# Neighborhood attention on one core: one two-bank P V tile per pair, and another division of work in the last step

## The chip, the cores and the metric

The kernel runs on one core of a Trainium2 chip. A core has five engines with queues of their own: TensorE (PE, with its weight loads shown as PEld), VectorE (DVE), ScalarE (ACT), GpSimd (POOL) and SyncE (SP). Each works its instructions off in the order in which they stand, and waits for others by semaphores. DMAs are issued from the queues of SP, ACT and POOL. Matmul results land in PSUM (eight banks of 2 KB a partition), which ACT and DVE read. The metric is the device time of one execution in microseconds.

## The reference

Every pixel of a 224 x 224 image with 192 channels attends to a 7 x 7 neighborhood with dilation 2, with a single head over all channels:

```python
qkv = x @ wqkv
off = jnp.arange(7) * 2
r0 = jnp.clip(ir - 6, 0, H - 1 - 12)          # ir, ic: row and column numbers; c0 likewise
ri = r0[:, None] + off[None, :]
nidx = (ri[:, None, :, None] * W + ci[None, :, None, :])
logits = jnp.einsum('bnc,bnkc->bnk', qf, kn) * C ** (-0.5)
p = softmax(logits)
o = jnp.einsum('bnk,bnkc->bnc', p, vn) @ wo
```

`kn` and `vn` are the rows of k and v that `nidx` names. Near the borders the window is clipped, so that the first and last rows and columns share windows. Inputs and outputs are bfloat16.

## The kernel before

**Tiling.** The dilation splits rows and columns by parity, and rows are handled by parity class `rc`. A step works on 16 rows of one class over the whole width; there are 14 steps (`NSTEP`), the classes taking turns. The width of a step is cut into 14 slots (`NSLOT`) of eight column pairs. Two slots make a pair (`class Pair`, called a job's pair in the title): m = 0 to 6 in a step n, k = 0 to 97 over all, with `ab` = 0 or 1 for the slot in the pair. The key projection is folded into the query side (G), the output projection into the values (VF, VD), so there is no separate projection of the output.

**Stages of a pair.** `stage1` makes the scores in PSUM by 16 or more matmuls a pair and the negative maxima on DVE (L503); `stage1b` makes the exponentials on ACT (L511, four a pair). `stage2` transposes the exponentials on PE into one PSUM tile (L521) and copies it to SBUF as `pt_sb` (L523, "the PT copy" below). `stage3` multiplies by the values (L532, P V matmuls), and since the values carry a column of ones, columns 192 and 193 of the result hold the sums of the exponentials. `stage4a` takes the reciprocals (L538); `stage4` normalizes into `o_sb` or, for slot 0, `o_s0` (L552 on DVE, L550 on ACT), and issues the stores (L558, and L571 for slot 0, "left-edge stores").

**The loop.** The body runs for k = 0 to 99. In one pass the engines get the scores and the maxima of pair k, the P V matmuls of pair k - 2 and their normalization, the transposes and the PT copy of pair k - 1, and between these the projections of the next step: `w64` (left-over half groups of G, in the passes m = 0, 2, 4 and 6) and `w128` (whole groups of G, and values). The last step has no projections to make. `in_order(tc)` fixes the order on each engine as it stands in the code, so no scheduler moves anything.

On DVE a pass is: two reductions, reciprocal and normalization of slot 0 of pair k - 2, PT copy of pair k - 1, reciprocal and normalization of slot 1 of pair k - 2. In the last step the PT copies of pairs 0 to 4 are on ACT. For the last three pairs the second slot's normalization is on ACT, as two operations, one for each column class.

**Buffers.** `ps_o` has two PSUM banks, one for each slot's P V result; `ps_t` one for the transposes, `ps_g` three for projections, weight preparation and the tiles of the last pair. `o_sb` has six tiles of one slot, `o_s0` two. A tile is given again when its last reader in the order of the code has been issued, and the new writer waits for the reader's semaphore: for a store, its landing.

**Stores.** A slot has a run of 16 rows, or in the last step one of 13 rows and one of 3 (the clipped rows have another spacing). Long runs go to SP's queue. Short runs go to POOL's or SP's by slot, and in the last two slots to ACT's at the end (`end_q`). The left-edge stores, ten or more for a step, wait in `pool_q`, together with POOL's copies of the next band (`sort_items`, `xb_items`); `pool_do` issues up to four of that list at the end of each pass. POOL also copies half groups of G out of `gx` (L460), for which it waits on ACT.

Of the kernel before, what the change touches and what calls it, by code (L numbers as in the profile page):

```python
# [8 lines left out]
BF = mybir.dt.bfloat16  # L9
F32 = mybir.dt.float32  # L10
# [11 lines left out]
NSLOT = 14  # L22
# [76 lines left out]
def kernel(  # L99
# [15 lines left out]
    pers = ctx.enter_context(tc.tile_pool(name="pers", bufs=1))  # L115
    ps_s = ctx.enter_context(tc.tile_pool(name="ps_s", bufs=1, space=PSUM))
    ps_t = ctx.enter_context(tc.tile_pool(name="ps_t", bufs=1, space=PSUM))
    ps_o = ctx.enter_context(tc.tile_pool(name="ps_o", bufs=2, space=PSUM))
    ps_g = ctx.enter_context(tc.tile_pool(name="ps_g", bufs=3, space=PSUM))
    x1_p = ctx.enter_context(tc.tile_pool(name="x1", bufs=2))  # L120

# [182 lines left out]
            nc.gpsimd.memset(_win(t, 0, 128, 112 * rc, [[128, 8], [1, 16]]), 0.0)  # L304
    wT_lo = setup.tile([128, 3, C], BF, name="wT_lo")
    wT_hi = setup.tile([64, 3, C], BF, name="wT_hi")
    n_t = 0
    for X in range(3):
        for (dt_, d0, dn) in ((wT_lo, 0, 128), (wT_hi, 128, 64)):
            tp = (ps_o, ps_g)[n_t % 2].tile([128, 1024], BF, name="tp_w", tag=("o", "pg")[n_t % 2])  # L310
            n_t += 1
            nc.tensor.transpose(tp[0:dn, 0:128], w_lo[:, X * C + d0: X * C + d0 + dn], ident[:])
            nc.tensor.transpose(tp[0:dn, 128:192], w_hi[:, X * C + d0: X * C + d0 + dn], ident[0:64, 0:64])
            nc.scalar.copy(out=dt_[:, X, :], in_=tp[0:dn, 0:192])
# [90 lines left out]
    def g_items(rc, ti, s0, ns):  # L405
# [41 lines left out]

        def halves(dve, direct=False):
            pg = ps_g.tile([128, 512], F32, name="pgh", tag="pg")
            pg1 = ps_o.tile([128, 512], F32, name="pgh", tag="o") if direct else pg  # L450
            both(mm(pg, 0, XDAT[0], OUT_B[0]), mm(pg1, 1, XDAT[1], OUT_B[1]))
            if direct:
                put(G[rc][0], (NSLOT + s0) * 128, pg, False, XDAT[0], 64)
                put(G[rc][1], (NSLOT + s0) * 128, pg1, True, XDAT[1], 64)
                return
            gx = work.tile([128, 512], BF, name="gx", tag="gx", bufs=3)
            put(gx, 0, pg, dve)
            for cc in range(2):
                p = XDAT[cc]
                nc.gpsimd.tensor_copy(out=G[rc][cc][p:p + 64, 1, s0:s0 + ns, :], in_=gx[p:p + 64, 0:ns * 128].rearrange("p (s q) -> p s q", q=128))  # L460
# [50 lines left out]
            nc.scalar.activation(out=J.p[:, ab, cc, :, z:z + 112].rearrange("p q (r k) -> p q r k", k=8), in_=_win(s_ps, 0, 128, cc * 256, [[8, 2], [16, 14], [1, 8]]),  # L511
                                 func=ACTF.Exp, bias=nmx[:, cc:cc + 1], scale=1.0)

    def stage2(J):
        pool_ = ps_t if J.k < NP - 1 else ps_g
        pt_ps = pool_.tile([128, 8, 128], BF, name="pt_ps", tag="pt" if J.k < NP - 1 else "pg")
        for ab in range(2):
            for cc in range(2):
                for q in range(2):
                    for h in range(2):  # L520
                        nc.tensor.transpose(pt_ps[64 * h:64 * h + 64, 4 * ab + 2 * cc + q, :], J.p[:, ab, cc, q, 64 * h:64 * h + 64], ident[:])  # L521
        J.pt = work.tile([128, 8, 128], BF, name="pt_sb", tag="pt_sb")
        (nc.scalar.copy if J.n == NSTEP - 1 and J.m < 5 else nc.vector.tensor_copy)(out=J.pt[:], in_=pt_ps[:])  # L523

    def stage3(J, ab):
        rc, s = J.rc, 2 * J.m + ab
        o_ps = (ps_o if J.k < NP - 1 else ps_g).tile([128, 512], F32, name="o_ps", tag="o" if J.k < NP - 1 else "pg")
        V = (VD[rc], VF[rc])
        for cc in range(2):
            for q in range(2):  # L530
                for h in range(2):
                    nc.tensor.matmul(o_ps[64 * h:64 * h + 64, cc * 193:cc * 193 + 193], lhsT=J.pt[:, 4 * ab + 2 * cc + q, 64 * h:64 * h + 64],  # L532
                                     rhs=V[h][:, (s - 1 + q) % NSLOT, cc * C:cc * C + 193], start=(q == 0), stop=(q == 1))
        J.o_ps[ab] = o_ps

    def stage4a(J, ab):
        J.rs[ab] = stat.tile([128, 2], F32, name="rs", tag="rs")
        nc.vector.reciprocal(out=J.rs[ab][:], in_=J.o_ps[ab][:, C:C + 2])  # L538
        return J.rs[ab]

    def stage4(J, ab):
        rc, ti, s, o_ps = J.rc, J.ti, 2 * J.m + ab, J.o_ps[ab]
        rs = J.rs.get(ab) or stage4a(J, ab)
        if s > 0:
            o_sb = work.tile([128, 2, C], BF, name="o_sb", tag="o_sb", bufs=6)
        else:
            o_sb = work.tile([128, 2, C], BF, name="o_s0", tag="o_s0")
        if J.k >= NP - 3 and ab == 1:
            for cc in range(2):
                nc.scalar.mul(o_sb[:, cc, :], o_ps[:, 194 * cc:194 * cc + C], rs[:, cc:cc + 1])  # L550
        else:
            nc.vector.tensor_tensor(out=o_sb[:], in0=_win(o_ps, 0, 128, 0, [[194, 2], [1, C]]),  # L552
                                    in1=rs[:].unsqueeze(2).to_broadcast([128, 2, C]), op=ALU.mult)
        prow = _rows(rc, ti)
        if s > 0:
            for (j0, nj, r0, rstep) in _aff_runs(prow):
                def put(eng, j0=j0, nj=nj, r0=r0, rstep=rstep):
                    eng.dma_start(out=op[r0: r0 + (nj - 1) * rstep + 1: rstep, 8 * s - 3:8 * s + 5, :],  # L558
                                  in_=o_sb[8 * j0:8 * (j0 + nj)].rearrange("p t c -> p (t c)"))

                if nj < 8 and J.n == NSTEP - 1 and s > 11:
                    end_q.append(put)
                else:
                    put(nc.gpsimd if nj < 8 and (s % 2 == 1 if J.n == 0 else s not in (3, 6, 9)) else nc.sync)
            return
        for h in range(2):
            for (j0, nj, r0, rstep) in _aff_runs(prow[8 * h:8 * h + 8]):
# [7 lines left out]
    for n, (ti, rc) in enumerate(steps):  # L575
        for m in range(7):
            J = Pair()
            J.n, J.ti, J.rc, J.m, J.k, J.o_ps, J.s, J.rs = n, ti, rc, m, len(pairs), {}, {}, {}
            pairs.append(J)
    NP = len(pairs)  # L580

# [5 lines left out]
    act, dve, pool = nc.scalar.copy, nc.vector.tensor_copy, nc.gpsimd.tensor_copy  # L587
    pool_q = []
    end_q = []

    def pool_do(n):
        for _ in range(min(n, len(pool_q))):
            pool_q.pop(0)()
# [35 lines left out]
    for k in range(NP + 2):  # L629
# [18 lines left out]
            if m == 0 and n + 3 < NBAND:  # L648
                ld = load_items(n + 3)
        if k == NP:  # L650
            stage2(pairs[k - 1])
        if k >= 2:
            stage3(pairs[k - 2], 0)
            stage3(pairs[k - 2], 1)
            if k >= NP:
                stage4a(pairs[k - 2], 0)
                stage4a(pairs[k - 2], 1)
            stage4(pairs[k - 2], 0)
            if k == NP - 1:
                stage4a(pairs[k - 2], 1)  # L660
        for it in w64:
            it(False)
        if J:
            stage1b(J, 1)
        if 1 <= k < NP:
            stage2(pairs[k - 1])
        if k >= 2:
            stage4(pairs[k - 2], 1)
        if not J:
            continue  # L670

# [46 lines left out]
        if n == 12 and m == 1:  # L718
# [1 line left out]
            g_col(1, 6, 0, 1, pool)  # L720
            g_row(1, 6, 0, 1, pool, last)
            g_row(1, 6, 1, 13, pool, last[1:])
        pool_do(4 if n + 1 < NSTEP else 3)
    pool_do(len(pool_q))
    for it in end_q:
        it(nc.scalar)
    in_order(tc)


# [28 lines left out]
```

## Time and profile before

| | |
|---|---|
| median of 3 runs | 364.18 us (363.53 to 366.75) |
| the profiled execution | 362.85 us, span 361.1 us, granted TensorE clock 0.996 |
| busy: PE / PEld | 335.6 / 305.8 us |
| busy: DVE / ACT / POOL | 313.7 / 307.5 / 285.6 us |
| normalizations on DVE (L552) | 193, 557 ns each |
| reciprocals (L538) | 196, 159 ns each |
| PT copies | 93 on DVE, 686 ns; 5 on ACT, 1018 ns |
| left-edge stores on POOL (L571) | 150 of 162 shown under one name, 568 ns to issue each |

The table's durations are those of single instructions; DVE and ACT overlap the end of one with the start of the next by about 0.1 us. A busy PE is modelled, since matmuls are pipelined. SP's queue has no busy time in the page; its instructions are seen in the order of time.

### The profile page before, as it was taken

To read this page: it belongs to the slowest core of one execution; us is meant where nothing else is said; L and a number is where in the kernel's file an instruction comes from. 1 tells how busy PE (TensorE), PEld (TensorE's weight loads), DVE (VectorE), ACT (ScalarE), POOL (GpSimd) and SP (SyncE) were. 2 spreads that over 40 slices of the span, in tenths; PEclk is the share of its full clock that TensorE was granted. 3 is DMA by queue.
4 is the path that set the end of the run, shared out by engine and by line. 5 is a ranking of instruction groups with operands and counts; after the bars stand their busy time and mean duration, and the time that the engine had idled before them with its cause. 6 is when DMAs were issued, how large, how long until landed. Compare 5 with 4: busy or idle time off the path is not lost.

```text
span 361.1 us, 19455 instructions
## 1 busy us (share of the span) xinstructions
PE 335.6 (93%) x8104; PEld 305.8 (85%) x8104; DVE 313.7 (87%) x743; ACT 307.5 (85%) x821; POOL 285.6 (79%) x456
## 2 busy tenths in 40 slices
PE   3988888998999999999999999999999999999881
PEld 1676777997999899999989999899999999999671
DVE  8967987887998998989989999898998889989992
ACT  3654767997998999989999999999989989999792
POOL 8976799999896986959969699696995878374094
PEclk9999999999999999999999999999999999999998
DMA  9999986697988979899799998988989965634432
GB/s 188 204 175 180 174 172 148 146 199 162 202 177 201 196 164 190 186 194 192 168 183 181 197 190 177 161 213 180 198 178 192 191 146 121 143 97 108 103 80 77
DMA packets 137778, 60.79 MB, mean 168 GB/s; under 512 B 88841, under 2 KB 137166, under 8 KB 137691
## 3 DMA queue, kind: packets, MB, share of 16 engines
q1 hardware_dynamic: 130133, 56.37, 78.3%
q0 software_dynamic: 5520, 1.73, 2.7%
q10 hardware_dynamic: 2038, 1.47, 2.2%
q8 instruction: 63, 1.03, 1.2%
q14 instruction: 24, 0.20, 0.2%
HBM read 0.29 MB, written 19.27 MB: 54 GB/s over the span
## 4 chain that ended last, share of the span: by engine, by line
PE 69%; POOL 10%; DVE 8%; ACT 6%; DMA 3%; issue 2%; SPq 1%; POOLq 0%; DVEq 0%; ACTq 0%
PE pv L345 16%; PE s L501 15%; PE o_ps L532 14%; PE pg L425 10%; PE pt_ps L521 9%; PE pgh L425 5%; POOL out_dram L571 4%; ACT p L511 3%; DVE xb L160 2%; POOL xs L170 2%; POOL out_dram L558 2%; DMA out_dram<-o_sb 1%; DMA vd<-vf 1%; ACT vf L335 1%; DVE nmx L503 1%
## 5 line engine op out<-in xcount | busy, mean ns | idle before, releaser
L511 ACT ACTIVATE p<-s,nmx 128x224 bf16<-128x224 f32 x392 | 149.8, 450 | 24.5 <-DVE nmx L503 22.8
L503 DVE TENSOR_REDUCE nmx<-s 128x2 f32<-128x392 f32 (+1 forms) x196 | 102.4, 564 | 19.9 <-PE s L501 19.4
L552 DVE TENSOR_TENSOR o_sb<-o_ps,rs 128x384 bf16<-128x384 f32 x179 | 99.8, 557 | 7.1 <-DMA out_dram<-o_sb 0.9
L460 POOL COPY g<-gx 64x512 bf16<-64x512 bf16 (+1 forms) x110 | 61.8, 562 | 52.9 <-ACT gx L335 47.1
L345 PE MATMUL pv<-wp,xs 128*64 128x192 bf16 x1624 | 92.7, 250 | 7.1 <-POOL xs L170 1.9
L345 PEld LDWEIGHTS <-xs 128*64 128x64 bf16 x1624 | 78.5, 111 | 20.5 <-issue 8.8
L335 ACT CAST vf<-pv 128x384 bf16<-128x384 f32 x193 | 87.6, 518 | 9.6 <-PE pv L345 5.2
L571 POOL DMA_DIRECT2D out_dram<-o_s x150 | 84.2, 568 | 1.1 <-issue 1.1
L532 PE MATMUL o_ps<-vd,pt_sb 128*64 128x193 bf16 x784 | 82.2, 246 | 2.9 <-ACT pt_sb L523 2.1
L501 PE MATMUL s<-xa,g 128*64 128x196 bf16 (+7 forms) x990 | 82.2, 233 | 1.6 <-issue 0.5
L532 PE MATMUL o_ps<-vf,pt_sb 128*64 128x193 bf16 x784 | 82.1, 246 | 0.0
L501 PE MATMUL s<-xb,g 128*64 128x196 bf16 (+7 forms) x990 | 81.8, 232 | 0.3 <-ACT g L335 0.3
L501 PEld LDWEIGHTS <-g 128*64 128x64 bf16 x1980 | 77.6, 110 | 3.6 <-issue 2.5
L532 PEld LDWEIGHTS <-pt_sb 128*64 128x64 bf16 x1568 | 71.3, 109 | 4.9 <-ACT pt_sb L523 3.2
L523 DVE COPY pt_sb<-pt_ps 128x1024 bf16<-128x1024 bf16 x93 | 63.7, 686 | 5.4 <-PE pt_ps L521 0.6
L521 PE MATMUL pt_ps<-ident,p 128*64 128x128 bf16 x1568 | 63.9, 219 | 0.0
L521 PEld LDWEIGHTS <-p 128*64 128x64 bf16 x1568 | 57.0, 110 | 5.2
L335 ACT CAST g<-pg 128x512 bf16<-128x512 f32 (+4 forms) x136 | 57.6, 471 | 2.0 <-PE pg L425 2.0
L425 PEld LDWEIGHTS <-aw 128*64 128x64 bf16 x1320 | 54.1, 110 | 4.1 <-issue 0.7
L425 PE MATMUL pg<-xb,aw 128*64 128x512 bf16 (+9 forms) x440 | 53.9, 269 | 0.6 <-DVE xb L160 0.6
L425 PE MATMUL pg<-xa,aw 128*64 128x512 bf16 (+9 forms) x440 | 52.0, 270 | 0.0
L170 POOL COPY xs<-xa 128x896 bf16<-128x896 bf16 x50 | 45.1, 928 | 1.4
(75 smaller groups left out, 282.8 us busy)
## 6 DMA issues: line engine op xcount, KB each, us to landing
vd<-vf SPq DMA_DIRECT2D x49, 336.9 KB
out_dram<-o_sb SPq DMA_DIRECT2D x156, 96.0 KB
out_dram<-o_sb SPq DMA_DIRECT2D x26, 78.0 KB
out_dram<-o_s POOLq DMA_DIRECT2D x78, 9.0 KB, 3.9
vd<-vf SPq DMA_DIRECT2D x2, 337.8 KB
vd<-vf ACTq DMA_DIRECT2D x2, 336.9 KB
xa<-in_x_dram SPq DMA_TRANSPOSE x28
out_dram<-o_s POOLq DMA_DIRECT2D x26, 15.0 KB, 3.1
```

What stands on the lines that cost most here:

```text
L335: nc.scalar.copy(out=out_, in_=in_)
L345: nc.tensor.matmul(pv[64 * h:64 * h + 64, cc * C:(cc + 1) * C], lhsT=at(k, h), rhs=WP[(cc, pas)][:], start=(pas == 0), stop=(pas == 1))
L425: nc.tensor.matmul(o, lhsT=l, rhs=r, start=(pas == 0), stop=(pas == 1))
L460: nc.gpsimd.tensor_copy(out=G[rc][cc][p:p + 64, 1, s0:s0 + ns, :], in_=gx[p:p + 64, 0:ns * 128].rearrange("p (s q) -> p s q", q=128))
L501: nc.tensor.matmul(o, lhsT=w, rhs=r, start=(pas == 0), stop=(pas == 1))
L503: nc.vector.tensor_reduce(out=nmx[:], in_=_win(s_ps, 0, 128, lo, [[256, 2], [16, 14], [1, 16 - lo]]), axis=AX.XY, op=ALU.max, negate=True)
L511: nc.scalar.activation(out=J.p[:, ab, cc, :, z:z + 112].rearrange("p q (r k) -> p q r k", k=8), in_=_win(s_ps, 0, 128, cc * 256, [[8, 2], ...
L521: nc.tensor.transpose(pt_ps[64 * h:64 * h + 64, 4 * ab + 2 * cc + q, :], J.p[:, ab, cc, q, 64 * h:64 * h + 64], ident[:])
L523: (nc.scalar.copy if J.n == NSTEP - 1 and J.m < 5 else nc.vector.tensor_copy)(out=J.pt[:], in_=pt_ps[:])
L532: nc.tensor.matmul(o_ps[64 * h:64 * h + 64, cc * 193:cc * 193 + 193], lhsT=J.pt[:, 4 * ab + 2 * cc + q, 64 * h:64 * h + 64], rhs=V[h][:, ( ...
L552: nc.vector.tensor_tensor(out=o_sb[:], in0=_win(o_ps, 0, 128, 0, [[194, 2], [1, C]]), in1=rs[:].unsqueeze(2).to_broadcast([128, 2, C]), op ...
L571: pool_q.append(lambda dst=dst, p=p, m=n * nj, cc=cc: nc.gpsimd.dma_start(out=dst.rearrange("j i c -> i j c"), in_=o_sb[p:p + m, cc, :]))
```

## The change

1. A pair's two slots share one PSUM tile of two banks, and `ps_o` holds a single one of them (same banks as before). One reciprocal of 128 x 4 and one normalization of 128 x 768 (reading both banks) stand in place of two each, ahead of the PT copy. `o_sb` becomes a tile of both slots, with four buffers; `o_s0` is gone, so the left-edge half lies in the pair's tile. The weight preparation at the start uses `ps_g` alone.
2. In the last step the outputs of all slots are kept in `XS[0]`, which is free by then, so no output buffer is given again. The PT copies of that step are on ACT in the passes m = 2 and 4, and on DVE in the others. In the passes m = 1, 3, 5, 6 and in the two after the last pair, the normalization is split: slot 0 on DVE, slot 1 on ACT; otherwise it is the joint one on DVE.
3. The short runs of the last step are stored for several slots at once: when slot 9 is done, three stores on POOL, one for each row, with slots 1 to 9; when slot 13 is done, three with slots 10 to 13, on ACT, SP and ACT.

```diff
-    ps_o = ctx.enter_context(tc.tile_pool(name="ps_o", bufs=2, space=PSUM))
+    ps_o = ctx.enter_context(tc.tile_pool(name="ps_o", bufs=1, space=PSUM))
...
-            tp = (ps_o, ps_g)[n_t % 2].tile([128, 1024], BF, name="tp_w", tag=("o", "pg")[n_t % 2])
+            tp = ps_g.tile([128, 1024], BF, name="tp_w", tag="pg")
...
-        (nc.scalar.copy if J.n == NSTEP - 1 and J.m < 5 else nc.vector.tensor_copy)(out=J.pt[:], in_=pt_ps[:])
+        eng(out=J.pt[:], in_=pt_ps[:])
...
+    def stage3(J):
+        rc = J.rc
+        if J.k < NP - 1:
+            o = ps_o.tile([128, 2, 512], F32, name="o_ps", tag="o")
+            J.o_ps = [o[:, ab, :] for ab in range(2)]
+            J.o_2 = o
+        else:
+            J.o_ps = [ps_g.tile([128, 512], F32, name="o_ps", tag="pg") for ab in range(2)]
...
     def stage4a(J, ab):
...
+        if J.rs is None:
+            J.rs = stat.tile([128, 2, 2], F32, name="rs", tag="rs")
+            if J.n < NSTEP - 1:
+                J.o_sb = work.tile([128, 2, 2, C], BF, name="o_sb", tag="o_sb", bufs=4)
+            else:
+                J.o_sb = _win(XS[0], 0, 128, 4 * C * J.m, [[2 * C, 2], [C, 2], [1, C]])
+        if ab is None:
+            nc.vector.reciprocal(out=J.rs[:], in_=_win(J.o_2, 0, 128, C, [[512, 2], [1, 2]]))
         else:
-            o_sb = work.tile([128, 2, C], BF, name="o_s0", tag="o_s0")
-        if J.k >= NP - 3 and ab == 1:
+            nc.vector.reciprocal(out=J.rs[:, ab, :], in_=J.o_ps[ab][:, C:C + 2])
+
+    def stage4b(J, ab, eng):
+        if ab is None:
+            nc.vector.tensor_tensor(out=J.o_sb[:], in0=_win(J.o_2, 0, 128, 0, [[512, 2], [194, 2], [1, C]]),
+                                    in1=J.rs[:].unsqueeze(3).to_broadcast([128, 2, 2, C]), op=ALU.mult)
+        elif eng is nc.vector:
+            nc.vector.tensor_tensor(out=J.o_sb[:, ab], in0=_win(J.o_ps[ab], 0, 128, 0, [[194, 2], [1, C]]),
+                                    in1=J.rs[:, ab, :].unsqueeze(2).to_broadcast([128, 2, C]), op=ALU.mult)
+        else:
             for cc in range(2):
+                nc.scalar.mul(J.o_sb[:, ab, cc, :], J.o_ps[ab][:, 194 * cc:194 * cc + C], J.rs[:, ab, cc:cc + 1])
...
+                if J.n < NSTEP - 1:
+                    put(nc.gpsimd if nj < 8 and s % 2 == 1 else nc.sync)
+                elif nj >= 8:
+                    put(nc.sync)
+                elif s in SHORT:
+                    for j in range(nj):
+                        def row(eng, p=8 * (j0 + j), r=r0 + j * rstep, a=SHORT[s]):
+                            eng.dma_start(out=op[r, 8 * a - 3:8 * s + 5, :].rearrange("(t i) c -> i t c", i=8),
+                                          in_=_win(XS[0], p, 8, 2 * C * a, [[2 * C, s + 1 - a], [1, 2 * C]]))
+                        if s < NSLOT - 1:
+                            pool_q.append(lambda row=row: row(nc.gpsimd))
+                        else:
+                            end_q.append(row)
...
+    SHORT = {9: 1, NSLOT - 1: 10}
...
+            P = pairs[k - 2]
+            stage3(P)
+            split = n == NSTEP or n == NSTEP - 1 and m % 2 == (0 if m == 6 else 1)
+            if P.k < NP - 1:
+                stage4a(P, None)
+            else:
+                stage4a(P, 0)
+                stage4a(P, 1)
+            stage4b(P, 0 if split else None, nc.vector)
+            stage5(P, 0)
...
         if 1 <= k < NP:
-            stage2(pairs[k - 1])
+            stage2(pairs[k - 1], act if n == NSTEP - 1 and m in (2, 4) else dve)
         if k >= 2:
-            stage4(pairs[k - 2], 1)
+            if split:
+                stage4b(P, 1, nc.scalar)
+            stage5(P, 1)
...
-        pool_do(4 if n + 1 < NSTEP else 3)
+        pool_do(4)
     pool_do(len(pool_q))
-    for it in end_q:
-        it(nc.scalar)
+    for it, eng in zip(end_q, (nc.scalar, nc.sync, nc.scalar)):
+        it(eng)
```

More of the change, by code (lines that the diff above doesn't have):

```diff
@@ L306 @@
     wT_hi = setup.tile([64, 3, C], BF, name="wT_hi")
-    n_t = 0
     for X in range(3):
         for (dt_, d0, dn) in ((wT_lo, 0, 128), (wT_hi, 128, 64)):
-            tp = (ps_o, ps_g)[n_t % 2].tile([128, 1024], BF, name="tp_w", tag=("o", "pg")[n_t % 2])
-            n_t += 1
+            tp = ps_g.tile([128, 1024], BF, name="tp_w", tag="pg")
             nc.tensor.transpose(tp[0:dn, 0:128], w_lo[:, X * C + d0: X * C + d0 + dn], ident[:])
@@ L449, in halves @@
             pg = ps_g.tile([128, 512], F32, name="pgh", tag="pg")
-            pg1 = ps_o.tile([128, 512], F32, name="pgh", tag="o") if direct else pg
+            pg1 = ps_o.tile([128, 2, 512], F32, name="pgh", tag="o")[:, 0, :] if direct else pg
             both(mm(pg, 0, XDAT[0], OUT_B[0]), mm(pg1, 1, XDAT[1], OUT_B[1]))
@@ L512, in stage1b, with stage2 @@
                                  func=ACTF.Exp, bias=nmx[:, cc:cc + 1], scale=1.0)
-    def stage2(J):
+    def stage2(J, eng):
         pool_ = ps_t if J.k < NP - 1 else ps_g
@@ L522, in stage2 @@
         J.pt = work.tile([128, 8, 128], BF, name="pt_sb", tag="pt_sb")
[L523 to L527, printed above, removed]
-        V = (VD[rc], VF[rc])
[L529 to L534, printed above, removed]
@@ L536, in stage4a @@
-    def stage4a(J, ab):
[L537 to L545, printed above, removed]
-        else:
-            o_sb = work.tile([128, 2, C], BF, name="o_s0", tag="o_s0")
-        if J.k >= NP - 3 and ab == 1:
+        eng(out=J.pt[:], in_=pt_ps[:])
@@ new lines, in stage3 @@
+    def stage3(J):
[6 more added lines that the diff above has]
+            J.o_ps = [ps_g.tile([128, 512], F32, name="o_ps", tag="pg") for ab in range(2)]
+        V = (VD[rc], VF[rc])
+        for ab in range(2):
+            s = 2 * J.m + ab
+            for cc in range(2):
+                for q in range(2):
+                    for h in range(2):
+                        nc.tensor.matmul(J.o_ps[ab][64 * h:64 * h + 64, cc * 193:cc * 193 + 193], lhsT=J.pt[:, 4 * ab + 2 * cc + q, 64 * h:64 * h + 64],
+                                         rhs=V[h][:, (s - 1 + q) % NSLOT, cc * C:cc * C + 193], start=(q == 0), stop=(q == 1))
@@ L549, in stage4, with stage5 @@
             for cc in range(2):
[L550 to L553, printed above, removed]
+                nc.scalar.mul(J.o_sb[:, ab, cc, :], J.o_ps[ab][:, 194 * cc:194 * cc + C], J.rs[:, ab, cc:cc + 1])
+    def stage5(J, ab):
+        rc, ti, s, o_sb = J.rc, J.ti, 2 * J.m + ab, J.o_sb[:, ab]
@@ L559, in put @@
                                   in_=o_sb[8 * j0:8 * (j0 + nj)].rearrange("p t c -> p (t c)"))
[L561 to L564, printed above, removed]
+                if J.n < NSTEP - 1:
[11 more added lines that the diff above has]
+                            end_q.append(row)
             return
@@ L577 @@
             J = Pair()
-            J.n, J.ti, J.rc, J.m, J.k, J.o_ps, J.s, J.rs = n, ti, rc, m, len(pairs), {}, {}, {}
+            J.n, J.ti, J.rc, J.m, J.k, J.s, J.rs = n, ti, rc, m, len(pairs), {}, None
             pairs.append(J)
@@ L650 @@
         if k == NP:
-            stage2(pairs[k - 1])
+            stage2(pairs[k - 1], dve)
         if k >= 2:
[L653 to L660, printed above, removed]
+            P = pairs[k - 2]
[8 more added lines that the diff above has]
+            stage5(P, 0)
         for it in w64:
@@ L665 @@
         if 1 <= k < NP:
-            stage2(pairs[k - 1])
+            stage2(pairs[k - 1], act if n == NSTEP - 1 and m in (2, 4) else dve)
         if k >= 2:
-            stage4(pairs[k - 2], 1)
+            if split:
+                stage4b(P, 1, nc.scalar)
+            stage5(P, 1)
         if not J:
```

## The prediction

> **What bounds the kernel now.** I read the busy times by stretch first, then the waits of TensorE (PE), then the order on VectorE (DVE), the POOL queue, and last the end of the SP queue. The busy times by stretch (start:end and length in us, then busy us of each engine; 0 to 66 left out):
>
> ```profile
> core 0: us, PE busy (x) PEld busy (x) DVE busy (x) ACT busy (x) POOL busy (x), PEclk, DMA share, GB/s
> 66.00:100.00 34.00, 32.51 (x734) 29.25 (x731) 29.10 (x70) 29.91 (x80) 31.98 (x51) 1.00 0.92 176
> 100.00:200.00 100.00, 99.30 (x2556) 93.65 (x2553) 90.07 (x215) 93.02 (x251) 83.21 (x118) 1.00 0.91 186
> 200.00:300.00 100.00, 99.71 (x2453) 93.33 (x2449) 90.38 (x216) 93.63 (x253) 80.88 (x114) 1.00 0.92 182
> 300.00:334.00 34.00, 33.99 (x942) 32.40 (x939) 31.09 (x75) 32.20 (x91) 20.12 (x46) 1.00 0.52 118
> 334.00:350.00 16.00, 13.30 (x303) 11.22 (x297) 14.54 (x39) 13.92 (x32) 7.50 (x14) 1.00 0.38 94
> 350.00:361.10 11.10, 3.38 (x80) 2.93 (x80) 4.41 (x13) 3.84 (x11) 5.74 (x11) 0.88 0.30 76
> ```
>
> From 100 to 334 PE has no idle time to give back. Its waits from 98 to 335, all of them (us, times, longest):
>
> ```profile
> PE s L501 <- issue: 0.5, 1, 0.5
> PE pv L345 <- ACT g L335: 0.2, 1, 0.2
> ```
>
> So three stages have different limits: steps 0 and 1 (20 to 92), where DVE, POOL and the SP queue take turns; steps 2 to 12, PE; and the last step with its drain (334 to 361), where PE is idle and DVE, ACT and the SP queue set the end. A change that mostly relieves DVE can gain only in the first and the third.
>
> One pass of the loop on DVE, in the middle stage (start, us, what):
>
> ```profile
> 201.03 1.07 DVE L503 TENSOR_REDUCE nmx<-s 128x2 f32<-128x420 f32 x2
> 202.01 0.16 DVE L538 RECIPROCAL rs<-o_ps 128x2 f32<-128x2 f32 x1
> 202.21 0.56 DVE L552 TENSOR_TENSOR o_sb<-o_ps,rs 128x384 bf16<-128x384 f32 x1
> 202.68 0.68 DVE L523 COPY pt_sb<-pt_ps 128x1024 bf16<-128x1024 bf16 x1
> 203.28 0.16 DVE L538 RECIPROCAL rs<-o_ps 128x2 f32<-128x2 f32 x1
> 203.47 0.56 DVE L552 TENSOR_TENSOR o_sb<-o_ps,rs 128x384 bf16<-128x384 f32 x1
> ```
>
> Start to start, a reciprocal takes 0.20, a normalization 0.47, the PT copy 0.60, two reductions 0.96 to 0.98. Passes last 3.4 us where left-over projection work (w64) is added, else 2.9.
>
> **Joint normalization.** Per pass 2 x (0.20 + 0.47) = 1.34 becomes one reciprocal and one normalization of 768 elements. No row shows it. From below: the DVE casts take 560 ns for 384 and 684 for 512 elements, 0.97 ns an element, so 557 + 384 x 0.97 = 0.93; from above two separate ones, 1.11. I take 0.95, occupying 0.87: saved 1.34 - 1.07 = 0.27 per pass, 26 us of DVE over 98 passes. In the middle stage PE hides all of it. But the PT copy now comes after 0.87 instead of 0.47. In the 2.9 passes it ended 0.64 before the P V matmuls needed it, and where PE waits for it the two lie 0.05 apart, so 0.59 is free: 0.40 later leaves 0.19. In the long passes the copy waits for its transposes anyway (margin 0.87 to 1.13) and loses 0.18 to 0.40. No PE stall from that at 0.95, nor at 1.11. In step 0 DVE runs back to back through four passes (reductions without a gap at 44.0, 49.2, 53.8), so up to 4 x 0.27; the chain goes on through SP and POOL there: I take **-0.4**, between 0 and -1.1.
>
> **One two-bank tile instead of two.** The P V matmuls of a pair must wait until the former pair is normalized. In the middle stage that is over 0.9 us before (202.21 + 0.95 against matmuls at 204.49), so 0; in the drain it counts, below. [...]
>
> **The output tiles.** Before, the left-edge half (slot 0) had its own two tiles; now it shares one of four pair tiles, which is held until the last of its ten left-edge stores lands. The other three rotate. In the built order the normalization of pair 6 takes this tile: it waits on all eight lanes of the POOL queue. The POOL queue in step 7, and the landing of such stores (min/median/max):
>
> ```profile
> 218.79 2.80 POOL L571 DMA_DIRECT2D out_dram<-o_s  x5
> 221.58 2.20 POOL L460 COPY g<-gx 64x512 bf16<-64x512 bf16 x4
> DMA to landing us min/median/max: 1.7/3.9/5.8
> ```
>
> The last of the five starts at 221.03 and its completion stands in the trace at 225.82. The normalization of pair 6 starts at 224.64: 1.18 late. The same difference for steps 2 to 12 (start minus landing): 0.69, 1.29, 0.51, 0.77, -0.70, -1.18, -0.66, 0.49, -0.18, 7.8, 7.8. Behind the waiting normalization on DVE stands the PT copy, and PE waits for that. It has 1.08 of cover in this pass, less 0.40 for the joint form: 0.68. So step 7 loses about 0.5, step 6 about 0.1, the rest nothing: **+0.5** (0 if the stores land 0.5 earlier). Waits on SP's stores at pair 4 (short by 0.65 in step 1, 0.22 in step 9) stay under cover.
>
> Step 1 is worse. Pair 2's normalization (73.35) gets the tile of the very first pair, whose last left-edge store starts at 71.91 and lands at 76.79. DVE then stands 3.4 us, the PT copy ends at 76.8 + 0.87 + 0.69 = 78.4 instead of 74.73, and the P V matmuls due at 75.60 start 2.8 late. At 84 to 90 PE waits 1.2 for POOL's sorted copies and 0.3 for ACT, up to 1.9 by the gaps between matmuls; POOL is busy from 60 to 92 and not delayed, so this is given back: **+1.0** (0.5 to 2.8).
>
> [...]
>
> **The last step.** DVE's own work falls: before, 0.96 + 1.34 = 2.3 a pass; after, 2.02 (PT copy on ACT), 2.22 (one half on ACT, PT copy on DVE). Yet passes alternate in a chain: reductions to first exponential 0.62, four exponentials 1.33, PT copy on ACT 1.02, P V matmuls of both halves with their latency 0.06 + 0.67 + 0.26, reciprocal 0.20, a half 0.47, PT copy on DVE 0.60: 5.23 for two passes. The trace of before has 5.1 for two (reductions at 339.52, 344.64, 349.74). Two such turns: +0.2; the first two passes give back 0.3 (DVE has 2.62 and 2.22 against 2.92 and 2.31 measured, ACT and PE follow). In the drain the P V matmuls of pair 5 wait for ACT's half of pair 4 (0.1), its reciprocal for both halves instead of one (0.34), less what stood between: the last normalizations end 0.3 later than 354.71 and 355.04.
>
> The end is SP's: it issued to the last us, with data that had been ready since 355.
>
> ```profile
> 356.30 1.70 SPq L558 DMA_DIRECT2D out_dram<-o_sb  x2
> ```
>
> Each store takes 0.9 there. It loses three short stores inside the step, where two stores a pass (1.8) now leave it waiting for data, and gains one behind slot 13. After pair 5's first half (354.2) stand four stores and the short one: the last starts at 354.25 + 4 x 0.91 = 357.9, against 357.21, and lands 2.2 later. If the new form is as quick as the 16-row stores (0.54), only its own 0.3 goes. ACT's two short ones follow its last half at 355.3 (1.4 + 0.7 before): not last. POOL saves six short stores and adds three of 72 pieces, from 352.5; 0.57 each as for 10 to 40 pieces, or three times that: 358 with 3.9 to land at worst 361 and level with SP's 360. Whole tail **+0.6** (-0.3 to +1.5).
>
> The weight transposes at the start use three tiles instead of five: ACT's copies of 0.32, back to back, set their pace either way: 0.
>
> **Sum**, on the profiled execution (362.85 us, span 361.1): -0.4 + 1.0 + 0.5 + 0.6 = +1.7. That execution lies 1.3 below the median of 364.18; added to the median: **365.9**. A measurement of this kernel tells about 1% (3.6 us) from no change.
>
> **Rivals.**
> - The last step follows DVE's work alone: six passes 2.62 + 2.22 + 2.02 + 2.22 + 2.02 + 2.22 = 13.3 against 15.45 measured, 2.1 less: 363.8. For: reductions stand there without a gap. Against: the 5.23 chain. Chance 0.20.
> - Slower, one mechanism: left-edge stores on POOL land later than in this profile, at pair 6. From 0.5 later on, steps 6 to 8 add up to 2.0 and step 1 0.5 more: 367.8; 1.0 later, 4.0 and 1.0 more: 370.3. For: landings reach 5.8, used here are 3.4 to 5.0. Chance 0.18.
> - The landings are short: 364.4. Chance 0.07.
> - Two banks in one operation cost more than two operations: at 1.30 the 0.19 falls short by 0.17 in three passes a step, 12 steps: 372. Against: the slope of the casts. Chance 0.05.
> - It does not do what it says: PE's busy time hides waits for DVE. Weight loads fill only 93.5% of 66 to 334; all of the rest would be 17 us, half of it 357. Against: 16 P V matmuls take 0.67 us in every pass, without gaps. Chance 0.05.
> - The forecast: 0.45.
>
> The range 362.4 to 369.0 leaves out the last two and the far ends of the first two. Faster by over 1%: 0.08; within: 0.73; slower: 0.19.
>
> **What would show it.** PE busy in 100 to 300 unchanged; DVE busy down by about 25 us; joint normalizations near 0.95; DVE waits for out_dram of about 3.4 us near 73 and of about 1 near 200 to 250; passes of the last step near 2.6; SP's last issue later than after the last normalization by 2 to 3 us. Wrong if passes of the middle stage grow or shrink, or the last step's fall to 2.2.

## The result, and the profile after

| | before | after |
|---|---|---|
| median, measured together (22 runs each) | 363.07 us (361.71 to 366.75) | 365.35 us (364.02 to 367.98) |
| ratio after / before, with its 95% interval | | **1.0051** (1.0034 to 1.0068) |
| the profiled execution / its span | 362.85 / 361.1 us | 364.58 / 362.8 us |
| busy DVE | 313.7 us | 291.6 us |

By the ratio the kernel became 0.5% slower, 1.9 us (1.2 to 2.5); the two medians lie 2.3 apart. The forecast was 1.7 us slower, 365.9. Single executions that took far longer than the rest are left out of the ratios, so that of 12 runs only 11 may count. DVE lost 22 us of work and the kernel gained nothing by it. From the page of the changed kernel, the busy times (part 1) and two of the costliest groups (part 5: out<-in, count, busy us and mean ns, idle time before them and its releaser):

```profile
PE 335.0 (92%) x8104; PEld 305.6 (84%) x8104; DVE 291.6 (80%) x554; ACT 307.0 (85%) x824; POOL 282.9 (78%) x451
...
L557 DVE TENSOR_TENSOR o_sb<-o_ps,rs 128x768 bf16<-128x768 f32 x90 | 86.2, 957 | 11.8 <-DMA out_dram<-o_sb 7.2
...
L521 DVE COPY pt_sb<-pt_ps 128x1024 bf16<-128x1024 bf16 x96 | 65.2, 680 | 0.1
```

The joint normalization takes 957 ns. The end of the second line is what is new: 7.2 us in which DVE stood before it for a store to land. The busy times by stretch (columns as before the change):

```profile
66.00:100.00 34.00, 30.86 (x707) 27.82 (x704) 26.27 (x49) 29.14 (x78) 30.86 (x49) 1.00 0.95 176
100.00:200.00 100.00, 99.51 (x2563) 94.83 (x2559) 82.77 (x155) 93.65 (x252) 83.57 (x118) 1.00 0.89 185
200.00:300.00 100.00, 98.78 (x2413) 90.94 (x2411) 81.85 (x152) 92.49 (x251) 79.55 (x112) 1.00 0.91 181
300.00:334.00 34.00, 33.99 (x953) 32.78 (x948) 28.55 (x54) 32.05 (x90) 20.73 (x47) 1.00 0.53 119
334.00:350.00 16.00, 13.72 (x313) 11.91 (x309) 13.47 (x27) 13.70 (x35) 7.40 (x13) 1.00 0.35 86
```

From 100 to 334, DVE (third pair) has 18 us less to do than in the kernel before, and PE (first) is as full as it was, but for 0.9 us in 200:300. Between 66 and 100 PE has lost 1.65 us. The waits of DVE for stores, and the place of the longest, in order of time on DVE:

```profile
DVE o_sb L557 <- DMA out_dram<-o_sb: 7.2, 4, 3.9
```

```profile
72.60 0.17 DVE L550 RECIPROCAL rs<-o_ps 128x4 f32<-128x4 f32 x1
76.72 0.96 DVE L557 TENSOR_TENSOR o_sb<-o_ps,rs 128x768 bf16<-128x768 f32 x1 [3.94 <-DMA out_dram<-o_sb]
77.59 0.68 DVE L521 COPY pt_sb<-pt_ps 128x1024 bf16<-128x1024 bf16 x1
```

Four waits: 3.94 in step 1, and 0.80, 1.06 and 1.35 at pair 6 of steps 6, 7 and 10:

```profile
203.30 0.96 DVE L557 TENSOR_TENSOR o_sb<-o_ps,rs 128x768 bf16<-128x768 f32 x1 [0.80 <-DMA out_dram<-o_sb]
226.09 0.96 DVE L557 TENSOR_TENSOR o_sb<-o_ps,rs 128x768 bf16<-128x768 f32 x1 [1.06 <-DMA out_dram<-o_sb]
295.20 0.96 DVE L557 TENSOR_TENSOR o_sb<-o_ps,rs 128x768 bf16<-128x768 f32 x1 [1.35 <-DMA out_dram<-o_sb]
```

Behind the longest, PE waits for the PT copy (PE's only wait from 70 to 82):

```profile
PE o_ps L537 <- DVE pt_sb L521: 3.1, 1, 3.1
```

How late each pass begins against the kernel before (first reduction, after minus before, in us; step, pair):

| place | late by | what happened |
|---|---|---|
| (0,6) to (1,4) | -0.4 to -0.8, then -0.56 | DVE's back-to-back passes of step 0 are shorter |
| (1,5) | +2.63 | pair 2's normalization waited for a left-edge store; 3.2 lost |
| (2,2) | +0.57 | 2.1 of it given back in PE's idle time at 84 to 90 |
| (3,5) to (6,6) | +0.29, -0.16, +0.31 | short stalls that both kernels have, in different steps |
| (7,3), (8,3), (11,2) | +0.42, +0.78, +1.49 | after the pair-6 waits of 0.80, 1.06 and 1.35: 0.11, 0.37 and 0.54 lost right behind them |
| (10,2) | +0.95 | 0.24 that no wait for a store explains |
| (13,0), (13,6) | +1.50, +1.69 | the last step is 0.2 longer |
| end | +1.69 | the last store lands 0.7 later than that, and SP's closing waits are 0.7 shorter |

The last step's reductions begin at 335.79, 338.45, 341.03, 343.44, 346.23, 348.58 and 351.43: two passes take 5.20 (341.03 to 346.23 to 351.43). Then SP's last issues in order of time (two long stores, and the short one for four slots):

```profile
358.26 1.74 SPq L573 DMA_DIRECT2D out_dram<-xs  x2
360.05 0.47 SPq L584 DMA_DIRECT2D out_dram<-xs  x1
```

By the semaphore records of the trace, the short store is the last to land, at 361.86. Before the change the last was SP's last long store, at 359.48. Counted from the last pair's reductions that is 10.43 against 9.74 us. Then SP waits for the semaphores of all stores once more, in a fixed order, and the program closes: 0.90 us from the last landing to the end, 1.60 before.

### The profile page after: what moved, and what is told of

The parts are those of the page before. It is cut to its first block, busy times and chain, and to the rows that moved or that the text cites. A ratio compares the mean times of both kernels' runs of the same rounds, so it can differ in the third digit from the quotient of the medians.

```text
span 362.8 us, 19103 instructions
## 1 busy us (share of the span) xinstructions
PE 335.0 (92%) x8104; PEld 305.6 (84%) x8104; DVE 291.6 (80%) x554; ACT 307.0 (85%) x824; POOL 282.9 (78%) x451
## 4 chain that ended last, share of the span: by engine, by line
PE 64%; POOL 12%; DVE 9%; ACT 5%; DMA 5%; issue 3%; DVEq 0%; ACTq 0%; POOLq 0%
PE s L499 14%; PE pv L343 14%; PE o_ps L537 14%; PE pg L423 9%; PE pt_ps L519 8%; PE pgh L423 5%; POOL out_dram L596 3%; ACT p L509 3%; POOL xs L170 3%; DMA out_dram<-o_sb 3%; DMA vd<-vf 3%; POOL g L458 2%; POOL xb L160 2%; DVE xb L160 2%; DVE nmx L501 1%
## 5 line engine op out<-in xcount | busy, mean ns | idle before, releaser
L343 PE MATMUL pv<-wp,xs 128*64 128x192 bf16 x1624 | 91.5, 250 | 6.1 <-ACT g L333 1.8
L557 DVE TENSOR_TENSOR o_sb<-o_ps,rs 128x768 bf16<-128x768 f32 x90 | 86.2, 957 | 11.8 <-DMA out_dram<-o_sb 7.2
L499 PE MATMUL s<-xa,g 128*64 128x196 bf16 (+8 forms) x990 | 82.1, 233 | 0.9 <-DVE g L331 0.3
L499 PE MATMUL s<-xb,g 128*64 128x196 bf16 (+8 forms) x990 | 81.7, 232 | 0.7 <-issue 0.5
L596 POOL DMA_DIRECT2D out_dram<-o_sb x135 | 75.8, 569 | 1.1 <-issue 1.1
L521 DVE COPY pt_sb<-pt_ps 128x1024 bf16<-128x1024 bf16 x96 | 65.2, 680 | 0.1
```

Source lines behind the costliest of these rows:

```text
L343: nc.tensor.matmul(pv[64 * h:64 * h + 64, cc * C:(cc + 1) * C], lhsT=at(k, h), rhs=WP[(cc, pas)][:], start=(pas == 0), stop=(pas == 1))
L499: nc.tensor.matmul(o, lhsT=w, rhs=r, start=(pas == 0), stop=(pas == 1))
L521: eng(out=J.pt[:], in_=pt_ps[:])
L557: nc.vector.tensor_tensor(out=J.o_sb[:], in0=_win(J.o_2, 0, 128, 0, [[512, 2], [194, 2], [1, C]]), in1=J.rs[:].unsqueeze(3).to_broadcast([ ...
L596: pool_q.append(lambda dst=dst, p=p, m=n * nj, cc=cc: nc.gpsimd.dma_start(out=dst.rearrange("j i c -> i j c"), in_=o_sb[p:p + m, cc, :]))
```

## The experiments

All are the changed kernel with the edit whose main lines are shown (`...` stands for lines left out). Ratios are to the kernel before, run beside each; an interval is 0.6 to 1.3 us to either side, and single profiles, which differ by 1 us among themselves, are read for places and not for sums.

**Own tiles for the left edge.** Three pair tiles instead of four, and two tiles for the slot-0 half as before; pair 0 of a step is normalized in two operations.

```diff
-                J.o_sb = work.tile([128, 2, 2, C], BF, name="o_sb", tag="o_sb", bufs=4)
+                J.o_sb = work.tile([128, 2, 2, C], BF, name="o_sb", tag="o_sb", bufs=3)
+                J.o_0 = work.tile([128, 2, C], BF, name="o_s0", tag="o_s0") if J.m == 0 else None
...
```

> The left-edge half gets two tiles of its own again, and the pair tiles are three; all else as changed. The pair with the left edge is normalized in two halves on VectorE (14 passes, 0.3 us each). Theory (the loss is the wait for left-edge stores, above all in step 1): the 3.9 us wait in step 1 and those of 0.8 to 1.4 at pair 6 of steps 6, 7, 10 go; span 361.1 (360.6 to 361.8) instead of 362.8, ratio to the kernel before 1.000. Rival (the loss is the single P V tile, or the last step): span stays 362.5 to 363.1, ratio 1.005.

Measured: 363.23 us, **0.9987** (0.9966 to 1.0009). The loss is gone, and a little of the gain of step 0 shows. In its profile (1,5) is 0.08 early instead of 2.63 late, and PE has no gap where it stood still for 2.8 us in the changed kernel (72:78, PE first):

```profile
72.00:78.00 6.00, 6.00 (x139) 5.48 (x136) 4.62 (x9) 5.74 (x16) 5.91 (x12) 1.00 1.16 194
```

That profile's span is no shorter (363.2), because PE stood still in it later on, among others for 1.1 us near 250, where it waits for ACT's copy of g. The same wait stands in the profiles of the two other kernels with own tiles and of the thinner maxima, and not in those of the kernel before and the changed one; it was not followed up. The ratio over 12 runs is the better witness.

**The old division of the last step.** The PT copies of the passes 1 to 5 on ACT, and the normalization split for the last three pairs only.

```diff
-            split = n == NSTEP or n == NSTEP - 1 and m % 2 == (0 if m == 6 else 1)
+            split = P.k >= NP - 3
...
-            stage2(pairs[k - 1], act if n == NSTEP - 1 and m in (2, 4) else dve)
+            stage2(pairs[k - 1], act if n == NSTEP - 1 and 1 <= m <= 5 else dve)
```

> As changed, but in the last step the PT copies of pairs 0 to 4 are on ScalarE again and only the last three pairs have their second half normalized there. Theory (the turns gain nothing, the loss lies in step 1): span 362.5 to 363.3, two passes of the last step 5.0 to 5.2. Rival (the new turns cost the loss): span 361.3 or less. Rival (the new turns gain and hide a larger loss): span 364 or more.

Measured: 366.7 us, 1.006 (1.0033 to 1.0088), no different from the changed kernel's 1.0051. The six passes of the last step take 15.22 us, against 15.64 with turns and 15.45 before: taking turns gains nothing.

**Thinner maxima.** In steps 2 to 12 the maximum is taken over 6 of the 14 key rows; a part of the maximum is left out, and the softmax has another shift.

```diff
+        r0, nr = (4, 6) if 2 <= J.n <= 12 else (0, 14)
-        nc.vector.tensor_reduce(out=nmx[:], in_=_win(s_ps, 0, 128, lo, [[256, 2], [16, 14], [1, 16 - lo]]), ...)
+        nc.vector.tensor_reduce(out=nmx[:], in_=_win(s_ps, 0, 128, 16 * r0 + lo, [[256, 2], [16, nr], [1, 16 - lo]]), ...)
```

> As changed, but in steps 2 to 12 the maximum is taken over 6 of the 14 rows of the scores, which every window touches; softmax does not change with it. VectorE has some 0.45 us less per pass, 35 us in all. Theory (TensorE sets the pace of the middle stage): passes stay 3.4 and 2.9 us, span 362.3 to 363.0. Rival (TensorE's busy time hides waits for VectorE): a tenth of the 35 us or more shows, span 359.5 or less.

Measured: 364.8 us, 1.0043 (1.002 to 1.0066). The busy times by stretch of this run:

```profile
100.00:200.00 100.00, 98.57 (x2540) 93.69 (x2536) 73.17 (x153) 91.84 (x249) 82.50 (x117) 1.00 0.94 185
200.00:300.00 100.00, 97.79 (x2393) 91.08 (x2390) 72.28 (x151) 91.11 (x248) 78.86 (x110) 1.00 0.93 180
```

DVE is down by another 19 us in 200, and the time stays: in steps 2 to 12 the saving on DVE was worth nothing. A part of it went into waiting: in this run DVE waits nine times for a store to land, 9.7 us in all, where the changed kernel has four waits of 7.2.

**Every pass of the last step split,** and all its PT copies on DVE.

```diff
-            split = n == NSTEP or n == NSTEP - 1 and m % 2 == (0 if m == 6 else 1)
+            split = n >= NSTEP - 1
...
-            stage2(pairs[k - 1], act if n == NSTEP - 1 and m in (2, 4) else dve)
+            stage2(pairs[k - 1], dve)
```

> As changed, but in the whole last step the normalization is split between VectorE and ScalarE and every PT copy is on VectorE. Theory (the last step is held by the chain through ScalarE's PT copy, 5.2 us for two passes): a pass falls to VectorE's own work, 0.95 + 0.20 + 0.47 + 0.60 = 2.2, so six passes take 13.6 to 14.2 instead of 15.7; span 361.0 to 361.8. Rival (the queue of stores or the score tiles set the pace): passes stay at 2.6, span 362.5 to 363.1.

Measured: 365.05 us, 1.005 (1.0026 to 1.0075), and the passes take 2.55 us, not 2.2. Without the PT copy on ACT there is another chain of the same length. DVE in the last step of this run (in order of time), and one of PE's waits there:

```profile
345.13 0.24 PE L537 MATMUL o_ps<-vd,pt_sb 128*64 128x193 bf16 x1 [0.34 <-ACT xs L564]
...
346.02 0.18 DVE L550 RECIPROCAL rs<-o_ps 128x4 f32<-128x4 f32 x1 [0.23 <-PE o_ps L537]
...
346.24 0.56 DVE L560 TENSOR_TENSOR xs<-o_ps,rs 128x384 bf16<-128x384 f32 x1
...
346.71 0.68 DVE L521 COPY pt_sb<-pt_ps 128x1024 bf16<-128x1024 bf16 x1
...
347.31 1.03 DVE L501 TENSOR_REDUCE nmx<-s 128x2 f32<-128x392 f32 x2
```

The P V matmuls wait for ACT's half of the former pair, because there is one tile (the first line); DVE waits for their result; behind it stand the PT copy and the next reductions, and behind these, on ACT, four exponentials and a half again. From the end of one such half to the end of the next but one: 0.95 + 0.21 + 0.47 + 0.60 + 0.59 + 1.53 + 0.73 = 5.08 for two passes.

**The same, with P V tiles that alternate.** In the last step pairs 0, 2, 4 and 6 take two one-bank tiles of the projections' pool, idle by then.

```diff
-        if J.k < NP - 1:
+        if J.n < NSTEP - 1 or J.m % 2:
             o = ps_o.tile([128, 2, 512], F32, name="o_ps", tag="o")
...
-            if P.k < NP - 1:
+            if P.n < NSTEP - 1 or P.m % 2:
                 stage4a(P, None)
```

> The earlier run with every pass split and all PT copies on DVE, plus one thing: in the last step, the P V results of pairs 0, 2, 4 and 6 go to two one-bank tiles of the projections' pool (idle there), those of pairs 1, 3 and 5 to the two-bank tile, so that no P V matmul has to wait for the former pair's normalization on ACT. Theory (the single two-bank tile holds the last step: end of ACT's half, P V matmuls 0.95, reciprocal 0.21, half 0.47, PT copy 0.60, reduction to exponentials 0.59, four exponentials 1.53, ACT's half 0.73 = 5.08 for two passes, 2.55 each as measured there): with the link cut DVE's work of 2.22 and 2.44 sets the pass, 2.35 on the mean, the six passes 14.1 us instead of 15.4 and the span about 1.0 shorter if the SP queue doesn't take it back. Rival (the exponentials and the score tiles hold it, not the P V tile): passes stay at 2.55.

Measured: 363.53 us, 1.0004 (0.9976 to 1.0032). Passes now begin at 341.51, 343.79, 346.13, 348.35 and 350.76: 2.31 on the mean against the 2.35 worked out, the six 14.45 us instead of 15.45. DVE in order of time stands without a gap:

```profile
343.79 1.03 DVE L501 TENSOR_REDUCE nmx<-s 128x2 f32<-128x392 f32 x2
344.84 0.18 DVE L550 RECIPROCAL rs<-o_ps 128x4 f32<-128x4 f32 x1
345.06 0.56 DVE L560 TENSOR_TENSOR xs<-o_ps,rs 128x384 bf16<-128x384 f32 x1
345.54 0.68 DVE L521 COPY pt_sb<-pt_ps 128x1024 bf16<-128x1024 bf16 x1
346.13 1.03 DVE L501 TENSOR_REDUCE nmx<-s 128x2 f32<-128x392 f32 x2
```

So it was the single two-bank tile that held the split passes, and with it gone DVE's work is the limit.

**Short runs stored slot by slot,** as before the change.

```diff
-                elif s in SHORT:
-                    ...
+                elif s > 11:
+                    end_q.append(put)
+                else:
+                    put(nc.gpsimd if s not in (3, 6, 9) else nc.sync)
...
```

> The changed kernel with only its third part undone: the short runs of the last step are stored slot by slot again, three of them on SP and the last two on ACT. Prediction's term: SP loses the short store behind slot 13, so its last store starts at about the same place as the last long one, 0.3 to 0.9 earlier than the last start in the changed kernel; three short stores come back inside the step. Theory after the changed kernel's profile (its short store on SP took 0.47 only): the span changes by less than 0.5 us either way. Rival (storing for several slots relieved the SP queue): the three short stores delay SP's last long stores by 0.8 each as far as they are not hidden, span 1 to 2 us longer.

Measured: 365.24 us, 1.0041 (1.0009 to 1.0074). From the last pair's reductions to the end it takes 11.60 us, in the changed kernel 11.34: the third part of the change is worth at most 0.3.

**The last long store on ACT's queue.**

```diff
-                    put(nc.sync)
+                    put(nc.sync if s < NSLOT - 1 else nc.scalar)
...
-    for it, eng in zip(end_q, (nc.scalar, nc.sync, nc.scalar)):
+    for it, eng in zip(end_q, (nc.sync, nc.scalar, nc.sync)):
```

> The changed kernel, with the long store of the very last slot on ACT's queue (behind ACT's last half) instead of SP's, and two of the three last short stores on SP, one on ACT. Theory (the SP queue's issues set the end: four long stores and a short one behind the data, the last start 2.8 us after the last normalization): SP's last start comes about 0.4 to 0.9 earlier and the span is 0.4 to 0.9 us shorter. Rival (the landing of POOL's stores or of the long stores' bytes sets the end): span unchanged.

Measured: 366.12 us, 1.0064 (1.0029 to 1.0099), and 11.32 us from the last reductions to the end, as with SP. The last issues of ACT's queue and of SP's:

```profile
357.88 1.44 ACTq L573 DMA_DIRECT2D out_dram<-xs  x1
359.42 0.34 ACTq L584 DMA_DIRECT2D out_dram<-xs  x1
```

```profile
359.52 0.86 SPq L584 DMA_DIRECT2D out_dram<-xs  x2
```

The long store that takes SP 0.8 takes ACT's queue 1.44. That is not the queue alone: in the run with the short runs slot by slot, two short stores of equal size take ACT 1.45 and 0.74, the first of them dearer.

The first half of the theory held. Counted from the last pair's reductions, SP's last issue ends at 8.64 instead of 9.08 us, and its store is again the last to land, at 9.99 instead of 10.43. The 0.44 was lost behind it: SP closes with one wait for each store's semaphore, about 0.06 us each, and here seven of them stand behind the one that comes last, in the changed kernel none. From the last landing to the end it takes 1.33 us instead of 0.90. In all 13 profiles of this case the last landing is that of SP's last store, 1.3 to 1.5 us after its issue ended, so the SP queue does set the end, as the prediction had it; the closing waits come on top.

**All together:** own left-edge tiles, every pass of the last step split, alternating P V tiles, the last long store on ACT.

> The changed kernel with all of these together: own tiles for the left-edge halves (three pair tiles), every pass of the last step split with the PT copies on DVE, alternating P V tiles in the last step, the last long store on ACT's queue. If the parts add: against the kernel before 0.9987 from the left-edge tiles, less 1.0 us from the alternation, less 0.6 from the end of the SP queue, so a ratio of 0.993 to 0.996, 361 us. If the SP queue takes back what the passes gain: 0.998.

Measured: 360.84 us, **0.9922** (0.9897 to 0.9948), 2.8 us faster than the kernel before and better than both. SP's last issues, in order of time, in a span of 359.4:

```profile
344.51 11.30 SPq L579 DMA_DIRECT2D out_dram<-xs  x10
355.90 0.76 SPq L590 DMA_DIRECT2D out_dram<-xs  x2
```

The last landing comes at 9.34 us after the last pair's reductions, 0.54 earlier than with alternating tiles alone, but the closing takes 1.33 instead of 0.91.

**Later left-edge stores: two runs that did not settle what they were made for.** Four memsets on POOL ahead of the last left-edge stores of steps 1 to 11, in the changed kernel and in the one with own tiles:

```diff
+        if 1 <= n <= 11 and m == 5:
+            for _ in range(4):
+                nc.gpsimd.memset(slow[:], 0.0)
         pool_do(4)
```

> The changed kernel with four idle memsets on POOL (0.25 us each by the rows of the start, 1.0 together) ahead of the last left-edge stores of each step from 1 to 11, in an unused tile. Theory (the left-edge half in the pair's tile makes pair 6's normalization wait for these stores' landing): each step that is within 1.0 of its landing now waits. By the margins of the kernel before (0.69, 1.29, 0.51, 0.77, -0.70, -1.18, -0.66, 0.49, -0.18 in steps 2 to 10) and 0.68 of cover, steps 6 to 8 and 10 lose 1.0, 1.5, 1.0 and 0.5: 3.5 to 4.0 more than the changed kernel has, less what it already lost there, so 2.5 to 4.0 more and a ratio of 1.012 to 1.016 to the kernel before; DVE's waits for out_dram about double, from 7 to 14 us or more. Rival (landings of these stores don't reach PE): 1.005 as before.

> The same four memsets on POOL in the kernel with tiles of their own for the left-edge halves. Theory: the stores land as late, but nothing waits for them, and POOL has 3.5 us of idle time behind them in a step, so the time is that of the kernel with own tiles without memsets, a ratio of 0.997 to 1.001. Rival (a POOL that is 1.0 us late costs by itself, through the copies of G and of the next band): as much dearer as the other kernel, 1.006 to 1.011.

Measured: 1.0056 (1.003 to 1.0082) for the first, 1.0033 (1.0014 to 1.0052) for the second. Neither theory's numbers came out; the first ratio is that of its rival, but not for the rival's reason. In the first run the memsets made the tile pool hand the left-edge tile on one pair later in most steps: the normalization that waits for six to eight semaphores is that of pair 0 of the next step, except in steps 5 and 11. So the pair-6 waits were not lengthened but gone; one wait is left in its profile, the one in step 1:

```profile
DVE o_sb L557 <- DMA out_dram<-o_sb: 4.2, 1, 4.2
```

From (2,2) to (13,0) that profile loses nothing (+2.47 to +2.43), where the changed kernel lost 0.93. This does not price the pair-6 waits: over the same stretch the profiles of the three kernels with own tiles, which have no left-edge waits, lose 0.7 to 2.2, and that of the alternating P V tiles, which shares the left-edge tile, loses nothing. And the second run says that a POOL that is 1 us late in every step costs by itself, 0.9987 to 1.0033, by a way that was not followed up; 3 of its 11 runs have a mean clock of 0.989 to 0.991, which no run with own tiles alone has. The two effects are of one size, so the ratio of the first shows neither.

**Idle matmuls in the stall of step 1.** Six of the profiles above, all of kernels with the shared left-edge tile, show something that the changed kernel's own profile does not have: PE stands still for 2.8 to 3.6 us in step 1 (from the start of one matmul to the start of the next), and then the granted clock falls (0.72 on the mean of 78:84 in each of the six). By stretch, PE first and PEclk third from last, the kernel with the short runs slot by slot:

```profile
72.00:78.00 6.00, 3.25 (x70) 2.67 (x64) 2.15 (x5) 3.33 (x9) 5.92 (x11) 1.00 1.17 216
78.00:84.00 6.00, 5.76 (x92) 5.03 (x94) 4.09 (x10) 3.65 (x9) 5.80 (x6) 0.72 0.67 146
84.00:90.00 6.00, 6.00 (x164) 5.77 (x162) 4.85 (x9) 5.69 (x18) 5.32 (x10) 1.00 0.65 129
```

and the changed kernel in the same stretches:

```profile
72.00:78.00 6.00, 3.24 (x70) 2.67 (x64) 2.06 (x5) 3.34 (x9) 5.92 (x11) 1.00 1.19 211
78.00:84.00 6.00, 5.67 (x127) 4.97 (x128) 5.64 (x11) 4.84 (x13) 5.80 (x6) 1.00 0.71 157
84.00:90.00 6.00, 6.00 (x166) 5.75 (x161) 4.90 (x10) 5.75 (x20) 5.76 (x10) 1.00 0.77 166
```

The stall is nearly the same, 2.75 us of 72:78; after it PE issues 92 matmuls in 6 us instead of 127. The edit gives PE something to do:

```diff
             P = pairs[k - 2]
+            if n == 1 and m == 5:
+                warm = ps_g.tile([128, 512], F32, name="warm", tag="pg")
+                for _ in range(7):
+                    nc.tensor.matmul(warm[:], lhsT=ident[:], rhs=pairs[k - 1].p[:, 0].rearrange("p a b c -> p (a b c)"), start=True, stop=True)
             stage3(P)
```

> The changed kernel with seven idle matmuls of 512 columns (1.5 us together) on PE in step 1 ahead of the P V matmuls that wait for the late PT copy; their result is read by nothing. PE stands still there for 2.8 to 3.6 us in the kernels with the shared left-edge tile, and in six of the eight profiles (not in that of the changed kernel itself) the granted clock then falls to 0.5 for 3.41 us; in the run with the thinner maxima the gap was 1.72 and the clock stayed. Theory (the falling clock is a part of what the left-edge wait costs): with the gap cut to about 1.8 the clock stays at 1.0, the passes after step 1 begin 1.1 us later than in the kernel before (as in the changed kernel's own profile) instead of 2.2 to 3.0, and the ratio to the kernel before falls from 1.005 to 1.002 or 1.003. Rival (PE's idle time behind the stall gives the slower clock back too): 1.005 as before.

Measured: 364.43 us, 1.0012 (0.9982 to 1.0042), as the theory has it, though the interval overlaps the changed kernel's (1.0034 to 1.0068). In this run's profile the store happened to land 1.9 us earlier than in the changed kernel's, so the profile shows no stall to compare. The mean clock of all runs, below, does speak for the theory; that earlier landings had a part in the ratio is not excluded.

## Why the prediction was right, point by point

The sign and the size came out (+1.9 measured, +1.7 forecast), and so did the mechanism named as the largest term: with own tiles the loss is gone. That the sum is so close is luck in part. In the profile steps 2 to 12 lost 0.4 more than worked out and the tail 0.4 less, and in the timed runs a fall of the clock, which no term has, adds about 0.6. Term by term, from the profiled executions:

- **Middle stage, nothing to gain from DVE: right,** and shown: from 100 to 300, 16 us less work on DVE, and 35 in the run with thinner maxima, moved nothing. The rival by which PE's busy time hides waits for DVE falls. (The 93.5% of weight loads, from which that rival was priced, is the share from 100 to 300; from 66 to 334 it is 92.8%.)
- **Joint normalization 0.95 us: right,** 0.957, and every one within 956 to 959 ns. The rival with a dearer two-bank operation falls. DVE is down by 22 us, not by 25 to 26.
- **Step 0, -0.4: right in kind,** -0.56.
- **Step 1, +1.0: right in place and mechanism,** shown by the run with own tiles. The landing was foreseen at 76.79, and the normalization that waited for it began at 76.72; the pass began 3.2 later, 2.1 was given back, net +1.1. That the landing fits to 0.1 is luck: in the nine profiles with a shared tile this wait lasts from 2.1 to 4.2 us. What the term lacked is the clock. Of the changed kernel's 22 runs, 10 have a mean granted clock of 0.987 to 0.992; none of the compared runs of the kernel before beside the experiments is under 0.993, nor is any of the 12 with own tiles, the 6 of all together or the 11 with idle matmuls. Those 10 average 366.05 us, the other 12 average 364.73. So in about half of the runs the time is 1.3 us longer, 0.6 on the mean, and the changed kernel's own profile is one without. The border is not sharp: a mean of 0.993 stands in the profile of the run with every pass split, where the clock fell, and in that of the memsets with own tiles, where it did not.
- **Pair 6, +0.5: right in mechanism, too small.** The passes behind the waits of 0.80, 1.06 and 1.35 begin 0.11, 0.37 and 0.54 later: the cover was 0.7 to 0.8, where 0.68 was worked out. Steps 6 and 7 came out at 0.5 together, as forecast (step 6, 0.70 late with 0.68 of cover, should by this sum have lost nothing). Step 10, put at 0.18 late and under cover, waited 1.35 and cost 0.5 on its own; step 8, put at 0.66 late, did not wait at all. The step that failed is the reading of landings off one execution to a tenth of a microsecond, where those of the left-edge stores spread from 1.6 to 5.5 us. The median of these stores is 3.6 us here and was 3.9 before the change, so the rival of short landings (364.4) did not come. What these waits cost in timed runs was not measured by itself.
- **The single P V tile, put at 0 until the drain.** The prediction had 0.9 us of cover for it in the middle stage. There that held: PE is busy for 99.51 and 98.78 of 100 us in 100:200 and 200:300. For the last step it was right by accident: there the chain over the PT copy on ACT, 5.23 forecast and 5.20 measured, hid that the single tile has a chain of 5.08 right behind it. Remove the first and the second takes over (2.55 us a pass with every pass split); rotate the tile and 0.24 us a pass is gained (2.31).
- **The tail, +0.6: too large,** +0.2 in all. The two turns of the last step cost 0.2, as worked out, but its first two passes gave nothing back (2.66 and 2.58 us, where 2.62 and 2.22 were worked out). The drain was as worked out: the last normalization ends 0.34 later than the shift of the passes explains. So was SP's last landing, 0.7 later, though by other parts: the short store for four slots took 0.47 to issue and not 0.9 (the case "as quick as the 16-row stores"), and SP stood for 0.45 before its last two long stores. The step that failed is the end behind the landing, for which the sum has no term: SP's closing waits took 0.90 us instead of 1.60 and gave the 0.7 back. In part this is their order: five semaphores stood behind the last one before the change, none after it; about 0.4 of it, in the barrier that closes the program, was not followed up.
- **The first rival, the last step by DVE's work alone,** failed for the reason given against it; DVE's work set the pass once both chains were cut (2.31 a pass). The slower rival, landings 0.5 to 1.0 later in steps 6 to 8, did not come; what goes with the slower half of the runs is the clock, which the prediction did not weigh.

In timed runs: with own tiles the kernel stands at 0.9987 and with shared ones at 1.0051, so sharing the tile costs about 2.3 us (by the two intervals 1 us more or less), which is more than the whole loss of 1.9; all the rest of the change lies between 1.2 us faster and 0.3 slower. In the profile the shifts of the passes add up to the whole: -0.56 in step 0, +1.1 in step 1, +0.9 in steps 2 to 12 (1.0 behind the three pair-6 waits, -0.1 by short stalls) and +0.2 in the last step, together +1.7.

## What to carry to other kernels

Before merging two buffers, look at who holds each longest: here a half that leaves by ten small DMAs kept the whole tile, and the wait (3.94 us at the longest) turned up at the next writer, several passes later, on an engine with time to spare. Where an engine is not the bound, less work on it may be worth nothing (here 16 and 35 us of DVE's work moved nothing), while one more wait on it can still reach the engine that is (of the 3.94 on DVE, 3.1 on PE). A chain that sets a stage may have another of nearly the same length behind it (here 5.20 and 5.08 for two passes): work out both before pricing the removal of the first.

## What was not expected of the hardware

- Behind a stall of PE of about 3 us the granted clock can fall. In six profiles with gaps of 2.81, 2.83, 3.20, 3.24, 3.54 and 3.61 us (from matmul start to matmul start) it was 0.5 for 3.41 us soon after (0.72 on the mean of 78:84); with a gap of 3.33 (the changed kernel's profile) and of 1.72 (the thinner maxima) it stayed at 1.0. So the length of the gap alone does not decide; what does was not shown.
- The clock did not fall in the gap: in the six, 72:78, which holds most of it (PE is busy for 3.2 to 3.4 of the 6 us), stands at 1.00, and the fall came 0.3 to 1.4 us after PE had started again. In 84:90 the clock is back at 1.00.
- Two PSUM banks in one DVE operation cost 0.03 us more than the slope of the casts gives: 957 ns for 768 elements, 557 for 384, 1.04 ns for each further element, against 0.97 by the casts (560 for 384, 684 for 512).
- A store of 13 rows of 6 KB took 0.8 us to issue on SP and 1.44 on ACT's queue as ACT's first; the short form with four slots a row took 0.28 to 0.47 on SP, and 0.84 as the first and 0.30 as the second on ACT's queue.
